# Sixteenth key tile of an attention head group: exponentials on VectorE instead of ScalarE, in a kernel of two attention layers and two token mixers

## The chip, the cores and the metric

The kernel runs on one core of a Trainium2 chip. The metric is the device time of one execution in microseconds. Six engines matter below. PE (TensorE) multiplies matrices and writes to PSUM, a memory of eight banks of 512 float32 columns on 128 partitions. ACT (ScalarE) and DVE (VectorE) work elementwise on PSUM and SBUF. POOL (GpSimd) works on SBUF and issues some DMAs, and SP (SyncE) issues the other DMAs. Each engine takes its instructions from a queue of its own, in order, and waits on semaphores that other engines set.

## The reference

```python
def _A_ref(x, wqkv, wo):              # B=1, S=2048, D=640, H=32, Dh=20
    qkv = ((x @ wqkv).reshape(B, S, 3, H, Dh)).transpose(2, 0, 3, 1, 4)
    q, k, v = qkv[0], qkv[1], qkv[2]
    scores = jnp.einsum("bhqd,bhkd->bhqk", q, k) * (Dh ** -0.5)
    p = _softmax(scores, axis=-1)
    o = jnp.einsum("bhqk,bhkd->bhqd", p, v)
    return o.transpose(0, 2, 1, 3).reshape(B, S, D) @ wo

def _B_ref(x, w1, b1, w2, b2):        # F=1536; mixes over the tokens
    h = _layernorm(x, axis=-1)
    u = _gelu(jnp.einsum("bsd,sf->bdf", h, w1) + b1)
    y = jnp.einsum("bdf,fs->bds", u, w2) + b2
    return y.transpose(0, 2, 1)

x = A_x
x = x + _A_ref(_layernorm(x), A_wqkv, A_wo)
x = x + _B_ref(_layernorm(x), B_w1, B_b1, B_w2, B_b2)
x = x + _A_ref(_layernorm(x), A_wqkv, A_wo)
x = x + _B_ref(_layernorm(x), B_w1, B_b1, B_w2, B_b2)
```

One attention layer needs 32 x 2048 x 2048 exponentials. The inputs are bfloat16.

## The kernel before

The program has four stages in a row: attention of layer 0, mixer 0, attention 1, mixer 1. The change touches the function `attention` and some constants at the top.

**Units and tiles.** The 32 heads are taken four at a time, in 8 head groups; the queries in 4 blocks of 512; the keys in 16 key tiles of 128. A unit is one (query block, head group, key tile), 512 units a layer. Each unit has four chunks, one for each head of the group: the scores of 128 keys by 512 queries, one PSUM bank. The chunks of all units, in order, are dealt out in threes to score tiles `S` of three banks; there are 683 of these a layer, and two buffers. The last tile of a layer has two chunks.

**What happens to a tile.** `emit_S` issues three matmuls, one a chunk. The head's 20 rows sit in one of four 32-row groups of PE (`tile_position`), and matmuls in different row groups run at the same time. `emit_exp` (line 322) takes the exponential of all three banks with one ACT instruction, [128, 1536], into a bfloat16 tile `P` (pool `ptp`, five buffers). No maximum is subtracted. `emit_PV` multiplies the four chunks of a unit with the values and adds them into the one `acc` bank over the 16 key tiles; the values carry a column of ones, which gives the softmax's denominators. After key tile 15, `normalize` (line 331) transposes `acc` on DVE in 32x32 blocks, takes reciprocals, multiplies and transposes back: four DVE instructions.

**The loop.** The loop at line 579 goes over the tiles. In iteration t it issues the scores of tile t+1, the exponential of tile t, the PV of every unit whose last chunk lies in tile t-1 or earlier, and then something to fill PE. `pe` (line 65) chains all PE instructions, so PE's order is the order of the program.

**What fills PE.** A queue of groups of matmuls holds the K and Q projections of the next head groups, the output projections and parts of the mixer's first matmul. `emit_fills` takes matmuls from it up to a budget: 3.0 of 512 columns in an iteration without PV, 1.5 in one with PV (the last may go over it, so two matmuls). A group writes the single `misc` bank; at its end DVE evacuates the bank, and for one iteration nothing is taken. For an output projection, the evacuation adds the residual, and after the second one of a row tile comes LN (`do_ln2`, line 357: two statistics, an aggregation, a small tensor-scalar, a power on POOL, an apply on DVE). In an iteration without fills, `keep_busy` (line 315) issues rounds of four matmuls with zero weights onto `acc`: SLOTS - 1 less the number of PVs.

**Order on the other engines.** The framework places the instructions of ACT, DVE, POOL and SP by data dependence and program order, and sets the semaphores. A tile's buffer is free for its next user when all its readers are done: a score tile when its exponential has read it.

Of the kernel before, what the change touches and what calls it, by code (L numbers as in the profile page):

```python
# [10 lines left out]

BF16 = mybir.dt.bfloat16
F32 = mybir.dt.float32
ACT = mybir.ActivationFunctionType
ALU = mybir.AluOpType
PSUM = bass.MemoryType.PSUM
# [5 lines left out]
NG = 8  # L22
# [6 lines left out]
    FILL_NOPV=3.0,  # L29
    FILL_PV=1.5,  # L30
    PV_LAGT=1,
    PT_BUFS=5,
    FILL_GAP=1,
    KQ_AHEAD=1,
    A0_LAG=2,
)


@with_exitstack
def kernel(  # L40
# [55 lines left out]
    nc.gpsimd.memset(zw[:], 0.0)  # L96
    zr = consts.tile([128, 512], BF16, name="zr")
    nc.gpsimd.memset(zr[:], 1.0)
    x1lp = ctx.enter_context(tc.tile_pool(name="x1lp", bufs=1))
    x1last = x1lp.tile([128, 4, D], F32, name="x1last")  # L100
    hhp = ctx.enter_context(tc.tile_pool(name="hhp", bufs=1))
# [141 lines left out]
    def attention(st, x_in_ap, x_mid, uacc_l):  # L243
        layer = st.layer
        KT, hT = st.KT, st.hT
        with ExitStack() as p1:
# [8 lines left out]
            h2_tiles = {}  # L255
            ptp = p1.enter_context(tc.tile_pool(name=f"ptp{layer}", bufs=CFG["PT_BUFS"]))
            atp = p1.enter_context(tc.tile_pool(name=f"atp{layer}", bufs=2))
            x1acc = {}
            LASTQB = NQB - 1
            PARTIAL_LAST = (NG % 2 == 0)  # L260
# [8 lines left out]
            tt_state = {}  # L269

            HORDER = (0, 1, 2, 3)
            chunks = [(n, j) for n in range(NU) for j in HORDER]
            NCH = len(chunks)
            NTILES = (NCH + 2) // 3

            def on_unit_start(n):
                qb_n, g_n, kt_n = units[n]
# [18 lines left out]
                if kt_n == 0:  # L296
                    ensure_ready(qb_n, g_n)

            def s_matmul(St, slot, n, j):
                qb, g, kt = units[n]  # L300
                pe(nc.tensor.matmul(St[:, slot, :], lhsT=KT[32 * j:32 * j + 32, g, kt * 128:(kt + 1) * 128],  # L301
                                    rhs=get_QT(st, qb)[32 * j:32 * j + 32, g, :], start=True, stop=True,
                                    tile_position=(32 * j, 0)))

            def emit_S(t):
                cs = chunks[3 * t:3 * t + 3]
                for (n, j) in cs:
# [4 lines left out]
                for i, (n, j) in enumerate(cs):  # L312
                    s_matmul(St, i, n, j)

            def keep_busy(count):
                for acc in acc_tiles.values():
# [4 lines left out]

            def emit_exp(t):
                St = S_tiles.pop(t)
                ncs = len(chunks[3 * t:3 * t + 3])
                P = ptp.tile([128, 3, 512], BF16, name="P")
                P_tiles[t] = P
                nc.scalar.activation(out=P[:, 0:ncs, :].rearrange("p a b -> p (a b)"),  # L327
                                     in_=St[:, 0:ncs, :].rearrange("p a b -> p (a b)"),
                                     func=ACT.Exp, scale=SCALE)
# [27 lines left out]
            def do_ln2(tt, x1s, engine):  # L357
                if tt >= 4 * MMO:
                    ln2_deferred.append((tt, x1s))
                    return  # L360
                mean, rstd = ln_stats(x1s[:], twice=True)
                h2t = h2sp.tile([128, D], BF16, name="h2st")
# [51 lines left out]
            def enqueue_outproj(qb):  # L414
                attnT = attnT_tiles[qb]
                for ttl in range(4):
                    tt = qb * 4 + ttl
                    for ci, (c0, c1) in enumerate(((0, 512), (512, D))):
                        w = c1 - c0
                        mms = []  # L420
                        for g in range(NG):
                            def mm(t, g=g, ttl=ttl, c0=c0, c1=c1, w=w, attnT=attnT, ci=ci, tt=tt):
                                if g == 0 and ci == 0:
                                    xin = xsp.tile([128, D], x_in_ap.dtype, name="xin")
                                    nc.sync.dma_start(out=xin[:], in_=x_in_ap[tt * 128:(tt + 1) * 128, :])
                                    tt_state[tt] = dict(xin=xin)
                                pe(nc.tensor.matmul(t[:, 0:w], lhsT=attnT[:, g, ttl * 128:(ttl + 1) * 128],  # L427
                                                    rhs=wo_pad[:, g, c0:c1], start=(g == 0), stop=(g == NG - 1)))
# [12 lines left out]
                        fill_queue.append(dict(mms=mms, evac=evac, cost=[1.0 if w > 256 else 0.35] * NG, key=("O", qb),  # L441
                                               not_before=fill_state["unit"] + 2))
# [73 lines left out]
            def emit_PV(n):  # L516
                qb, g, kt = units[n]
                if kt == 0:
                    acc_tiles[(qb, g)] = accp.tile([128, 512], F32, name="acc")
                acc = acc_tiles[(qb, g)]  # L520
                for j in range(4):
                    ci = 4 * n + HORDER.index(j)
                    P = P_tiles[ci // 3]
                    hh = 4 * g + j
                    pe(nc.tensor.matmul(acc[32 * j:32 * j + 32, :],  # L525
                                        lhsT=Vaug[:, (kt * H + hh) * VW:(kt * H + hh) * VW + 32],
                                        rhs=P[:, ci % 3, :], start=(kt == 0), stop=(kt == NKT - 1),
                                        tile_position=(0, 32 * j)))
                for t_ in list(P_tiles.keys()):
                    if (3 * t_ + 2) // 4 <= n:  # L530
                        del P_tiles[t_]
                if kt == NKT - 1:
                    normalize(qb, g, acc_tiles.pop((qb, g)))
                    if qb == LASTQB and PARTIAL_LAST:
                        if g % 2 == 1:
                            enqueue_outproj_partial(qb, g)
                    elif g == NG - 1:
                        enqueue_outproj(qb)

            def emit_fills(budget, pool_alloc):  # L540
# [5 lines left out]
                while spent < budget:  # L546
                    if fs["cur"] is None:
                        if not fill_queue:
                            break
                        if fill_queue[0].get("not_before", 0) > fs["unit"] and budget < 100:  # L550
                            break
                        fs["cur"] = fill_queue.popleft()
                        fs["idx"] = 0
                        fs["tile"] = pool_alloc()
                    grp = fs["cur"]
                    grp["mms"][fs["idx"]](fs["tile"])
                    spent += grp["cost"][fs["idx"]]
                    fs["idx"] += 1
                    if fs["idx"] == len(grp["mms"]):
                        grp["evac"](fs["tile"])  # L560
                        fs["cur"] = None
                        fs["cooldown"] = CFG["FILL_GAP"]
                        break
# [275 lines left out]
```

## Time and profile before

| | us |
|---|---|
| median of 3 runs | 2100.99 (2099.99 to 2101.32) |
| the profiled execution's own time | 2096.18 |
| its span, first to last instruction | 2094.4 |
| ACT busy | 1927.4 |
| of it line 327, the exponentials | 1835.9 |
| PE busy (its matmuls overlap; ends are modelled) | 1739.4 |
| DVE busy | 528.0 |
| POOL busy | 148.2 |

The profile gives busy time for each engine over one execution, groups of instructions by source line and shape, a chain of waits followed back from the last instruction, and the single instructions in order of time. The duration of an instruction in a group is from its own start to its own end; instructions that follow each other closely on one engine overlap, so that the busy time of a group is less than its count times its mean. The attention stages reach from about 49 to 963 us and from about 1090 to 2009 us; the mixers lie behind each. The granted PE clock was 0.985 on average.

### The profile page before, as it was taken

The numbers are of one execution on the slowest core, as the hardware profiler recorded it, in microseconds if no ns is written. First come the engines' busy times: TensorE is split into PE (matmuls) and PEld (weight loads), VectorE is DVE, ScalarE is ACT, GpSimd is POOL, SyncE is SP. The second block draws the span as 40 slices with busy tenths as digits, with TensorE's granted clock in tenths as the row PEclk, the third lists the DMA queues.
The fourth block names the chain that finished last, engine by engine and source line by source line (L and its number), as shares of the span: only waits on it lengthen the run. The fifth ranks groups of instructions, "written<-read, shape, count | busy, mean of one in ns | idle before, by whom it ended". The sixth has DMA issues, their size and how long they took to land.

```text
span 2094.4 us, 38271 instructions
## 1 busy us (share of the span) xinstructions
PE 1739.4 (83%) x16568; PEld 658.0 (31%) x16568; DVE 528.0 (25%) x1095; ACT 1927.4 (92%) x1504; POOL 148.2 (7%) x220
## 2 busy tenths in 40 slices
PE   7888888888888888887998888888888888878779
PEld 4222222232223322323542222222322223223235
DVE  6122222211321022213642122222112220322242
ACT  5999999999999999996449999999999999999962
POOL 2000000110012001110000000001100120011000
PEclk9999999999999999998999999999999999999999
DMA  5000000110034002223620000001101340132145
GB/s 130 1 1 1 1 20 20 61 54 11 29 59 71 2 29 43 41 30 106 221 85 1 1 1 1 26 27 66 48 14 39 65 65 1 52 53 38 20 140 182
DMA packets 90760, 97.27 MB, mean 46 GB/s; under 512 B 9696, under 2 KB 68192, under 8 KB 90592
## 3 DMA queue, kind: packets, MB, share of 16 engines
q1 hardware_dynamic: 70464, 71.22, 10.8%
q0 software_dynamic: 20128, 23.62, 7.5%
q8 instruction: 129, 2.11, 0.4%
q14 instruction: 39, 0.32, 0.0%
HBM read 55.48 MB, written 39.32 MB: 45 GB/s over the span
## 4 chain that ended last, share of the span: by engine, by line
ACT 68%; issue 17%; PE 12%; DVE 2%; DMA 1%; POOL 0%; SPq 0%; DVEq 0%; ACTq 0%; POOLq 0%
ACT P L327 67%; PE y L721 5%; PE S L301 1%; PE pp L217 1%; PE acc L525 1%; PE big L650 1%; PE misc L226 1%; DMA ua<-uacc 1%; PE misc L400 1%; PE acc L319 0%; PE pp L226 0%; PE S L460 0%; DMA x0in<-in_A_x_dram 0%; DVE bnst L157 0%; DVE x1last L473 0%
## 5 line engine op out<-in xcount | busy, mean ns | idle before, releaser
L327 ACT ACTIVATE P<-S 128x1536 bf16<-128x1536 f32 (+1 forms) x1366 | 1835.9, 1888 | 5.5 <-PE S L301 5.3
L301 PE MATMUL S<-QTq,KT 32*128 32x512 bf16 x4096 | 541.0, 383 | 314.0 <-ACT P L327 284.8
L301 PEld LDWEIGHTS <-KT 32*128 32x128 bf16 x4096 | 243.5, 91 | 796.5 <-issue 759.6
L525 PE MATMUL acc<-P,Vaug 128*32 128x512 bf16 x4096 | 414.1, 393 | 0.8 <-DVE T L336 0.5
L319 PE MATMUL acc<-zr,zw 128*32 128x512 bf16 x5208 | 390.5, 383 | 0.0
L525 PEld LDWEIGHTS <-Vaug 128*32 128x32 bf16 x4096 | 105.6, 93 | 235.9 <-issue 235.2
L319 PEld LDWEIGHTS <-zw 128*32 128x32 bf16 x5208 | 129.6, 96 | 90.9 <-issue 26.5
L406 DVE COPY ustg<-misc 128x512 f32<-128x512 f32 (+1 forms) x144 | 70.0, 486 | 335.6 <-PE misc L400 335.3
L336 DVE STREAM_TRANSPOSE T<-acc 128x512 f32<-128x512 f32 x64 | 45.8, 716 | 389.3 <-PE acc L525 389.1
L168 POOL TENSOR_TENSOR rstd<-veps,mhalf 128x1 f32<-128x1 f32 x64 | 35.4, 553 | 1180.0 <-DVE veps L163 1061.8
L400 PE MATMUL misc<-h2st,w1st 128*128 128x512 bf16 (+1 forms) x576 | 118.6, 308 | 0.0
L411 POOL DMA_DIRECT2D uacc<-ustg x96 | 82.6, 860 | 471.9 <-DVE ustg L406 443.0
L721 PE MATMUL y<-uT,w2s 128*128 128x512 bf16 (+1 forms) x768 | 107.7, 299 | 2.8 <-ACT uT L664 2.8
L487 DVE CAST QTq<-misc 128x512 bf16<-128x512 f32 x62 | 42.8, 691 | 243.3 <-PE misc L226 243.3
L226 PE MATMUL misc<-hh,wq_pad 128*128 128x512 bf16 x310 | 100.4, 391 | 0.0
L487 DVE CAST KT<-misc 128x512 bf16<-128x512 f32 x56 | 38.7, 690 | 217.9 <-PE misc L226 217.9
L226 PE MATMUL misc<-hh,wk_pad 128*128 128x512 bf16 x280 | 87.1, 385 | 0.0
L427 PE MATMUL misc<-wo_pad,attnT 128*128 128x512 bf16 (+1 forms) x384 | 77.3, 304 | 0.0
L721 PEld LDWEIGHTS <-w2s 128*128 128x128 bf16 x768 | 59.7, 98 | 49.1 <-issue 4.3
L76 ACT CAST Vaug<-pp 128x500 bf16<-128x500 f32 (+1 forms) x32 | 14.3, 452 | 51.3 <-PE pp L217 51.3
L436 DVE TENSOR_TENSOR x1s<-misc,xin 128x512 f32<-128x512 f32 (+1 forms) x48 | 23.5, 489 | 148.6 <-PE misc L427 148.5
L217 PE MATMUL pp<-wv,hh 128*128 128x500 bf16 (+1 forms) x320 | 50.4, 307 | 1.6 <-DVE hh L78 1.6
(76 smaller groups left out, 690.1 us busy)
## 6 DMA issues: line engine op xcount, KB each, us to landing
uacc<-ustg POOLq DMA_DIRECT2D x72, 256.0 KB, 4.0
w2s<-in_B_w_dram SPq DMA_DIRECT2D x16, 768.0 KB
w1st<-in_B_w_dram SPq DMA_DIRECT2D x36, 256.0 KB
xd<-x1s SPq DMA_DIRECT2D x24, 320.0 KB
x1in<-xd SPq DMA_DIRECT2D x24, 320.0 KB
ua<-uacc SPq DMA_DIRECT2D x24, 320.0 KB
xd<-x2s SPq DMA_DIRECT2D x16, 320.0 KB
xin<-xd SPq DMA_DIRECT2D x16, 320.0 KB
```

The lines of the kernel that those rows point to most:

```text
L217: pe(nc.tensor.matmul(pp[:, 0:c1 - c0], lhsT=st.hT[:, dt_, tt * 128:(tt + 1) * 128], rhs=wv[:, dt_, c0:c1], start=(dt_ == 0), stop=(dt_ == ...
L226: pe(nc.tensor.matmul(t[:, :], lhsT=wpad[:, dt_, g, :], rhs=st.hT[:, dt_, tb * 512:(tb + 1) * 512], start=(dt_ == 0), stop=(dt_ == NDT - 1)))
L301: pe(nc.tensor.matmul(St[:, slot, :], lhsT=KT[32 * j:32 * j + 32, g, kt * 128:(kt + 1) * 128], rhs=get_QT(st, qb)[32 * j:32 * j + 32, g, : ...
L319: pe(nc.tensor.matmul(acc[32 * j:32 * j + 32, :], lhsT=zw[:], rhs=zr[:], start=False, stop=False, skip_group_check=True, tile_position=(0, ...
L327: nc.scalar.activation(out=P[:, 0:ncs, :].rearrange("p a b -> p (a b)"), in_=St[:, 0:ncs, :].rearrange("p a b -> p (a b)"), func=ACT.Exp, ...
L400: pe(nc.tensor.matmul(t[:, 0:w], lhsT=states[fp]["w"][:, sti, ftl * 128:(ftl + 1) * 128], rhs=tiles4[sti][:, c0:c1], start=(sti == 0), sto ...
L406: nc.vector.tensor_copy(out=stg[:, 0:w], in_=t[:, 0:w])
L411: nc.gpsimd.dma_start(out=dst, in_=stg[:, 0:w], accum_op=ALU.add)
L427: pe(nc.tensor.matmul(t[:, 0:w], lhsT=attnT[:, g, ttl * 128:(ttl + 1) * 128], rhs=wo_pad[:, g, c0:c1], start=(g == 0), stop=(g == NG - 1)))
L487: nc.vector.tensor_copy(out=dst_ap, in_=t[:, :])
L525: pe(nc.tensor.matmul(acc[32 * j:32 * j + 32, :], lhsT=Vaug[:, (kt * H + hh) * VW:(kt * H + hh) * VW + 32], rhs=P[:, ci % 3, :], start=(kt ...
L721: pe(nc.tensor.matmul(y[:, 0:w], lhsT=w2s[:, ft, sl * 128:(sl + 1) * 128], rhs=uT[:, ft, c0:c1], start=(ft == 0), stop=(ft == NF - 1)))
```

## The change

In every head group and query block, key tile 15 (`VE_UNITS`) no longer goes to ACT. Its four chunks are put one by one into the third bank of score tiles early in the same group, three tiles apart (`VE_SPACING`); these mixed tiles have only two chunks for ACT, and `emit_exp` then covers two banks. In the mixed bank a matmul with constant weights `cw` first writes a bias, and the score matmul adds to it. DVE reads the bank once (`ve_first`): it multiplies by scale x log2(e) x 2^23, cuts at zero and writes int32. These bits, read as a float, hold the exponent. For each pair of such banks five more DVE instructions on 1024 columns follow (`ve_enqueue`): two bitwise ones separate mantissa and exponent, and three with two tensors evaluate a cubic polynomial of the mantissa, times the exponent, into a bfloat16 tile `Pd` that PV reads. They are held in a deque and issued by `ve_step` at an iteration's end, when an estimated clock of DVE says that it is free within 0.3 us; `ve_flush` issues what is left ahead of the unit's PV.

Besides, `P` has four buffers instead of five; next to mixed tiles one keep-busy round is left out, and the fill budget is 1.5; PV goes by the last tile of a unit (`last_tile`); and in layer 1 the sum `x1s` is written over the loaded residual `xin`.

```diff
-    PT_BUFS=5,
+    PT_BUFS=4,
+    VE_UNITS=((15,),),
+    VE_SPACING=3,
+    VE_SLACK=0.3,
...
+    ve_scale = SCALE * LOG2E
+    ve_bias = (127.0 + EXP_SHIFT) / ve_scale
+    cw = consts.tile([128, 128], BF16, name="cw")
+    nc.gpsimd.memset(cw[:], 0.0)
+    left = ve_bias
+    for row in (0, 32, 64):
...
+        nc.gpsimd.memset(cw[row:row + 1, :], part)
...
+            vew = p1.enter_context(tc.tile_pool(name=f"vew{layer}", bufs=2))
+            vet = p1.enter_context(tc.tile_pool(name=f"vet{layer}", bufs=1))
+            vep = p1.enter_context(tc.tile_pool(name=f"vep{layer}", bufs=2))
...
-            chunks = [(n, j) for n in range(NU) for j in HORDER]
...
+            act_chunks = deque((n, j) for n in range(NU) for j in HORDER if not is_ve[n])
...
+            while act_chunks or ve_queue:
+                if act_chunks:
+                    qb_, g_, _ = units[act_chunks[0][0]]
+                    if seen_group != (qb_, g_):
+                        seen_group = (qb_, g_)
+                        n0 = (qb_ * NG + g_) * NKT
+                        ve_queue += [(n0 + kt, j) for kt in ve_kts(qb_, g_) for j in HORDER]
+                t = len(tiles)
+                ve = None
+                na = 3
+                if ve_queue and t - last_mixed >= CFG["VE_SPACING"]:
+                    js = {c[1] for c in list(act_chunks)[:2]}
+                    ve = next((c for c in ve_queue if c[1] not in js), ve_queue[0])
+                    ve_queue.remove(ve)
+                    last_mixed = t
+                    na = 2
+                acts = [act_chunks.popleft() for _ in range(min(na, len(act_chunks)))]
...
+            def ve_first(p, slot, St):
+                if slot == 0:
+                    ve_w[p] = vew.tile([128, 2, 512], I32, name="ew")
+                nc.vector.tensor_scalar(out=ve_w[p][:, slot, :], in0=St[:, 2, :], scalar1=ve_scale * 2.0 ** 23,
+                                        scalar2=0.0, op0=ALU.mult, op1=ALU.max)
+                dve_cost(0.69)
+                if slot + 1 == len(ve_pairs[p]):
+                    ve_enqueue(p)
+
+            def ve_enqueue(p):
...
+                def mant():
+                    box["m"] = vet.tile([128, 1024], I32, name="em")
+                    nc.vector.tensor_scalar(out=box["m"][:, 0:512 * k], in0=wi, scalar1=0x007FFFFF, scalar2=0x3F800000,
+                                            op0=ALU.bitwise_and, op1=ALU.bitwise_or)
...
+                def expo():
+                    nc.vector.tensor_scalar(out=wi, in0=wi, scalar1=0x7F800000, scalar2=None, op0=ALU.bitwise_and)
+
+                def p1_():
+                    box["t"] = vet.tile([128, 1024], F32, name="et")
+                    nc.vector.scalar_tensor_tensor(out=box["t"][:, 0:512 * k], in0=box["mf"], scalar=EXP_A, in1=box["mf"],
+                                                   op0=ALU.add, op1=ALU.mult)
...
+                    nc.vector.scalar_tensor_tensor(out=t, in0=t, scalar=EXP_B, in1=box["mf"], op0=ALU.add, op1=ALU.mult)
...
+                    Pd = vep.tile([128, 2, 512], BF16, name="Pd")
+                    ve_P[p] = Pd
+                    nc.vector.scalar_tensor_tensor(out=Pd[:, 0:k, :].rearrange("p a b -> p (a b)"),
+                                                   in0=box["t"][:, 0:512 * k], scalar=EXP_C, in1=wf,
+                                                   op0=ALU.add, op1=ALU.mult)
+                for cost, fn in ((0.69, mant), (0.69, expo), (1.22, p1_), (1.22, p2_), (1.22, p3_)):
+                    ve_chain.append((p, cost, fn))
+
+            def ve_step(us):
+                ve_clock["now"] += us
+                while ve_chain and ve_clock["free"] <= ve_clock["now"] + CFG["VE_SLACK"]:
+                    p, cost, fn = ve_chain.popleft()
+                    fn()
+                    dve_cost(cost)
...
             def emit_S(t):
...
                 St = sps.tile([128, 3, 512], F32, name="S")
                 S_tiles[t] = St
+                if ve is not None:
+                    pe(nc.tensor.matmul(St[:, 2, :], lhsT=cw[:], rhs=zr[:], start=True, stop=False,
+                                        skip_group_check=True))
+                for i, (n, j) in enumerate(acts):
                     s_matmul(St, i, n, j)
+                if ve is not None:
+                    s_matmul(St, 2, ve[0], ve[1], start=False)
+                    ve_first(*loc[ve], St)
...
-                                ts_["x1s"] = xsp.tile([128, D], F32, name="x1s")
+                                ts_["x1s"] = (ts_["xin"] if x_in_ap.dtype == F32 else
+                                              xsp.tile([128, D], F32, name="x1s"))
...
+                if is_ve[n]:
+                    ve_flush(n)
                 for j in range(4):
-                    ci = 4 * n + HORDER.index(j)
-                    P = P_tiles[ci // 3]
+                    ti, slot = loc[(n, j)]
+                    P = ve_P[ti] if is_ve[n] else P_tiles[ti]
...
-                while pv_done < NU and (4 * pv_done + 3) // 3 <= t - LAGT:
+                while pv_done < NU and last_tile[pv_done] <= t - LAGT:
...
+                short = len(tiles[t][0]) < 3
+                extra = 1 if t + 1 < NTILES and tiles[t + 1][1] is not None else 0
                 if not has_fill:
-                    keep_busy(CFG["SLOTS"] - 1 - n_pv)
-                emit_fills(CFG["FILL_PV"] if n_pv else CFG["FILL_NOPV"], misc_alloc)
+                    keep_busy(CFG["SLOTS"] - 1 - n_pv - extra - short)
+                emit_fills(CFG["FILL_PV"] if n_pv or extra or short else CFG["FILL_NOPV"], misc_alloc)
+                ve_step(0.92 if short else 1.344)
```

More of the change, by code (lines that the diff above doesn't have):

```diff
@@ L13 @@
 F32 = mybir.dt.float32
+I32 = mybir.dt.int32
 ACT = mybir.ActivationFunctionType
@@ L35 @@
     A0_LAG=2,
-)
+    VE_UNITS=((15,),),
+    VE_SPACING=3,
+    VE_SLACK=0.3,
+)
+LOG2E = 1.4426950408889634
+EXP_C3 = 0.07802455
+EXP_A = -0.00800647 / EXP_C3
+EXP_B = 0.47777278 / EXP_C3
+EXP_C = 0.45213437 / EXP_C3
+EXP_SHIFT = float(np.log2(EXP_C3))
 @with_exitstack
@@ L98 @@
     nc.gpsimd.memset(zr[:], 1.0)
+    ve_scale = SCALE * LOG2E
[4 more added lines that the diff above has]
+    for row in (0, 32, 64):
+        part = float((np.asarray(left, np.float32).view(np.uint32) & np.uint32(0xFFFF0000)).view(np.float32))
+        nc.gpsimd.memset(cw[row:row + 1, :], part)
+        left -= part
     x1lp = ctx.enter_context(tc.tile_pool(name="x1lp", bufs=1))
@@ L271, in attention, with ve_kts @@
             HORDER = (0, 1, 2, 3)
-            chunks = [(n, j) for n in range(NU) for j in HORDER]
-            NCH = len(chunks)
-            NTILES = (NCH + 2) // 3
+            def ve_kts(qb, g):
+                pat = CFG["VE_UNITS"]
+                return pat[(qb * NG + g) % len(pat)]
+            is_ve = [kt in ve_kts(qb, g) for (qb, g, kt) in units]
+            tiles, loc, last_tile = [], {}, {}
+            ve_queue, ve_pairs = [], []
+            act_chunks = deque((n, j) for n in range(NU) for j in HORDER if not is_ve[n])
@@ new lines, in attention @@
+            last_mixed = -CFG["VE_SPACING"]
+            seen_group = None
+            while act_chunks or ve_queue:
[15 more added lines that the diff above has]
+                acts = [act_chunks.popleft() for _ in range(min(na, len(act_chunks)))]
+                for i, c in enumerate(acts):
+                    loc[c] = (t, i)
+                    last_tile[c[0]] = t
+                if ve is not None:
+                    if not ve_pairs or len(ve_pairs[-1]) == 2:
+                        ve_pairs.append([])
+                    loc[ve] = (len(ve_pairs) - 1, len(ve_pairs[-1]))
+                    ve_pairs[-1].append(ve)
+                    last_tile[ve[0]] = t
+                tiles.append((acts, ve))
@@ new lines, in attention, with dve_cost @@
+            NTILES = len(tiles)
+            ve_w, ve_P = {}, {}
+            ve_chain = deque()
+            ve_clock = dict(now=0.0, free=0.0)
+            def dve_cost(us):
+                ve_clock["free"] = max(ve_clock["free"], ve_clock["now"]) + us
+            def ve_first(p, slot, St):
[6 more added lines that the diff above has]
+                    ve_enqueue(p)
@@ new lines, in ve_enqueue, with p2_, p3_ @@
+            def ve_enqueue(p):
+                k = len(ve_pairs[p])
+                w = ve_w.pop(p)
+                wi = w[:, 0:k, :].rearrange("p a b -> p (a b)")
+                wf = wi.bitcast(F32)
+                box = {}
+                def mant():
+                    box["m"] = vet.tile([128, 1024], I32, name="em")
+                    nc.vector.tensor_scalar(out=box["m"][:, 0:512 * k], in0=wi, scalar1=0x007FFFFF, scalar2=0x3F800000,
+                                            op0=ALU.bitwise_and, op1=ALU.bitwise_or)
+                    box["mf"] = box["m"][:, 0:512 * k].bitcast(F32)
+                def expo():
[4 more added lines that the diff above has]
+                                                   op0=ALU.add, op1=ALU.mult)
+                def p2_():
+                    t = box["t"][:, 0:512 * k]
+                    nc.vector.scalar_tensor_tensor(out=t, in0=t, scalar=EXP_B, in1=box["mf"], op0=ALU.add, op1=ALU.mult)
+                def p3_():
+                    Pd = vep.tile([128, 2, 512], BF16, name="Pd")
[5 more added lines that the diff above has]
+                    ve_chain.append((p, cost, fn))
@@ new lines, in ve_step, with ve_flush @@
+            def ve_step(us):
[4 more added lines that the diff above has]
+                    dve_cost(cost)
+            def ve_flush(n):
+                need = {loc[(n, j)][0] for j in HORDER}
+                while any(c[0] in need for c in ve_chain):
+                    p, cost, fn = ve_chain.popleft()
+                    fn()
+                    dve_cost(cost)
@@ L297, in on_unit_start, with s_matmul @@
                     ensure_ready(qb_n, g_n)
-            def s_matmul(St, slot, n, j):
+            def s_matmul(St, slot, n, j, start=True):
                 qb, g, kt = units[n]
                 pe(nc.tensor.matmul(St[:, slot, :], lhsT=KT[32 * j:32 * j + 32, g, kt * 128:(kt + 1) * 128],
-                                    rhs=get_QT(st, qb)[32 * j:32 * j + 32, g, :], start=True, stop=True,
-                                    tile_position=(32 * j, 0)))
+                                    rhs=get_QT(st, qb)[32 * j:32 * j + 32, g, :], start=start, stop=True,
+                                    skip_group_check=not start, tile_position=(32 * j, 0)))
             def emit_S(t):
-                cs = chunks[3 * t:3 * t + 3]
-                for (n, j) in cs:
+                acts, ve = tiles[t]
+                for (n, j) in acts:
                     if j == HORDER[0]:
@@ L311, in emit_S @@
                 S_tiles[t] = St
-                for i, (n, j) in enumerate(cs):
+                if ve is not None:
+                    pe(nc.tensor.matmul(St[:, 2, :], lhsT=cw[:], rhs=zr[:], start=True, stop=False,
+                                        skip_group_check=True))
+                for i, (n, j) in enumerate(acts):
                     s_matmul(St, i, n, j)
+                if ve is not None:
+                    s_matmul(St, 2, ve[0], ve[1], start=False)
+                    ve_first(*loc[ve], St)
             def keep_busy(count):
@@ L323, in emit_exp @@
                 St = S_tiles.pop(t)
-                ncs = len(chunks[3 * t:3 * t + 3])
+                ncs = len(tiles[t][0])
+                if ncs == 0:
+                    return
                 P = ptp.tile([128, 3, 512], BF16, name="P")
@@ L361, in do_ln2 @@
                 mean, rstd = ln_stats(x1s[:], twice=True)
+                dve_cost(2.0)
                 h2t = h2sp.tile([128, D], BF16, name="h2st")
@@ L526, in emit_PV @@
                                         lhsT=Vaug[:, (kt * H + hh) * VW:(kt * H + hh) * VW + 32],
-                                        rhs=P[:, ci % 3, :], start=(kt == 0), stop=(kt == NKT - 1),
+                                        rhs=P[:, slot, :], start=(kt == 0), stop=(kt == NKT - 1),
                                         tile_position=(0, 32 * j)))
-                for t_ in list(P_tiles.keys()):
-                    if (3 * t_ + 2) // 4 <= n:
-                        del P_tiles[t_]
+                if not is_ve[n]:
+                    for t_ in list(P_tiles.keys()):
+                        if tiles[t_][0][-1][0] <= n:
+                            del P_tiles[t_]
                 if kt == NKT - 1:
                     normalize(qb, g, acc_tiles.pop((qb, g)))
+                    dve_cost(2.4)
                     if qb == LASTQB and PARTIAL_LAST:
@@ L560, in emit_fills @@
                         grp["evac"](fs["tile"])
+                        dve_cost(grp.get("dve", 0.69))
                         fs["cur"] = None
```

## The prediction

> **What bounds the kernel now.** I read the page's busy shares first, then its groups by shape, the chain, the waits, the busy time by stretch, and last two stretches of the timeline.
>
> ```profile
> PE 1739.4 (83%) x16568; PEld 658.0 (31%) x16568; DVE 528.0 (25%) x1095; ACT 1927.4 (92%) x1504; POOL 148.2 (7%) x220
> ...
> ACT 68%; issue 17%; PE 12%; DVE 2%; DMA 1%; POOL 0%; SPq 0%; DVEq 0%; ACTq 0%; POOLq 0%
> ```
> ```profile
> L327 ACT ACTIVATE P<-S 128x1536 bf16<-128x1536 f32 x1364 | 1834.1, 1888 | 5.5 <-PE S L301 5.3
> ...
> L341 DVE TENSOR_TENSOR T<-T,rden 128x512 bf16<-128x512 f32 x64 | 44.2, 691 | 2.1
> ...
> L487 DVE CAST KT<-misc 128x512 bf16<-128x512 f32 x56 | 38.7, 690 | 217.9 <-PE misc L226 217.9
> ...
> L173 DVE TENSOR_SCALAR h2st<-x1s,mv,rstd 128x640 bf16<-128x640 f32 x24 | 14.7, 613 | 17.5 <-POOL rstd L168 17.5
> ...
> L76 ACT CAST Vaug<-pp 128x500 bf16<-128x500 f32 x19 | 10.7, 574 | 25.8 <-PE pp L217 25.8
> ...
> L76 ACT CAST Vaug<-pp 128x140 bf16<-128x140 f32 x13 | 3.6, 275 | 25.4 <-PE pp L217 25.4
> ...
> L327 ACT ACTIVATE P<-S 128x1024 bf16<-128x1024 f32 x2 | 3.2, 1597 | 0.0
> ```
> ```profile
> PE S L301 <- ACT P L327: 284.8, 937, 0.9
> ```
> ```profile
> 280.00:510.00 230.00, 191.26 (x1903) 67.74 (x1901) 48.43 (x94) 229.40 (x172) 15.20 (x28) 0.99 0.11 35
> ```
> The exponentials own the two attention stages: 1366 of them keep ACT busy 1835.9 us, 1.344 us a tile (their 1888 ns overlap), and they wait 5.5 us in all. PE waits for them 937 times. The last row holds a stretch's length and then PE, weight loads, DVE, ACT and POOL: ACT has 229.4 of 230 us, DVE 48.4. Over the eight attention stretches read so, DVE has 387.6 of 1828 us, 21%. What ACT loses in work here comes off the end, as long as PE and DVE keep up.
>
> PE's room shows in this stretch (start, length):
> ```profile
> 515.23 0.39 PE L301 MATMUL S<-QTq,KT 32*128 32x512 bf16 x3
> 515.55 0.10 PEld L525 LDWEIGHTS <-Vaug 128*32 128x32 bf16 x4 [0.23 <-issue]
> 515.55 0.40 PE L525 MATMUL acc<-P,Vaug 128*32 128x512 bf16 x4
> 515.88 0.11 PEld L427 LDWEIGHTS <-attnT 128*128 128x128 bf16 x2 [0.23 <-issue]
> 515.88 0.60 PE L427 MATMUL misc<-wo_pad,attnT 128*128 128x512 bf16 x2
> 516.42 0.23 PEld L301 LDWEIGHTS <-KT 32*128 32x128 bf16 x3 [0.42 <-issue]
> ```
> From start to start: scores 0.32, PV 0.33, two fill matmuls 0.54, together 1.19 of 1.344 us. Elsewhere in that stretch three fills take 0.76 and two keep-busy rounds with their PV 0.76.
>
> **Removed: ACT work.** Counting through the new tile loop: still 683 tiles a layer, but 128 are mixed, with two banks for ACT and one for DVE. Both layers lose 512 columns from 256 exponentials. What is 512 columns worth? The two casts give (574-275)/360 = 0.83 ns a column, 0.425 us; a third of the period would be 0.448; the 1024-wide exponentials are 0.291 shorter by the means, and 0.467 by their minimum (1445 ns) against the median (1912 ns). The casts' slope is the only one free of queueing, so 0.425: 256 x 0.425 = 108.8 us (ends 74.5 and 119.6). A short exponential then takes 0.92 us.
>
> **Added: DVE work.** For each mixed tile one read of a score bank, 0.69 by the KT cast, same shape and source. For each pair of such tiles five operations on 1024 columns. The three with two tensors: the 512-column tensor-tensor row is 0.691; between the 512 and 128-column copies out of PSUM (0.685, 0.288) lies 1.03 ns a column, so 0.691 + 0.53 = 1.22. The two bitwise ones have no row. The nearest is the f32 tensor-scalar, 0.613 for 640: unchanged it bounds them below, the two-tensor 1.22 above; scaled by columns it gives 0.98, and I take 0.80. A pair: 2 x 0.69 + 2 x 0.80 + 3 x 1.22 = 6.64 us (6.27 to 7.48); 128 pairs: 850 us. With the 387.6 that is 1238 us in some 1730 us of attention: 72% (69 to 78). It fits, beside ACT.
>
> The Trainium skill, "ScalarE: Activation LUTs", Rules for kernel authors, speaks against the change: for exp, ScalarE is the only option. The rows bear out that DVE is the dear place, 3.3 us a bank against 0.43 on ACT; by the rule the sum would be 256 x (3.3 - 0.43), 735 us worse, were both on one path. They aren't: ACT is full and DVE 79% idle.
>
> **Added: waits on DVE's queue.** The bank read waits for its score matmul, and evacuations, normalize and LN stand behind it. S two tiles later waits for it. Scores of mixed tile m start when exponential m-2 ends and the banks are needed again 1.344 + 0.92 = 2.26 us later. Bias and scores take 0.71, the read 0.69: 0.86 us spare before PE is held, and about 0.85 more (1.344 less S's 0.39 and a handover) before ACT runs dry. A chain operation in front (1.22) fits into 1.71. What does not: LN of a row tile (two statistics 0.98, aggregation 0.20, veps 0.15, POOL 0.55, apply 0.61, handovers: some 3 us behind its 0.69 evacuation). Of the 12 a layer, two stand one tile ahead of a mixed one: 4 x 1.5 = 6 us at most. Normalize always stands two tiles ahead; its transpose frees the only acc buffer, and a chain operation in front makes the next PV late by up to 1.22, mostly within S's spare. A late misc evacuation holds the next fill: at 1135.05 it starts 2.59 us ahead of that fill, so 1.9 spare, 1.5 with a short tile between. For all of this 5 us (0 to 30).
>
> The skill's "SBUF — State Buffer", on the shared port of DVE and GpSimd, says that a two-port DVE operation shuts POOL out of writing DMA descriptors for its whole length; no run here shows it. Counted as 0.8 us for each of the 144 uacc issues that is 115 us on POOL, which is 7% busy, and nothing at the end.
>
> **Added: PE work.** A bias matmul in front of the scores (0.22 after a fill, 0.32 after keep-busy, by the steps above), and in 64 of the 128 tiles the DVE bank shares its row group with one of the other two, so the three no longer run at once: 0.22. Taken off: keep-busy rounds next to mixed tiles. Counting iterations through the loop, a layer: ahead of a mixed tile 25 with fills alone (1.08), 33 with fills and PV (1.41), 69 without fills (1.17 to 1.19), and 0.11 for the shared row groups: 1.33 on average; at the mixed one 58 at 1.19, 18 with two PVs at 1.42, 52 with one keep-busy round or none at 0.86: 1.09; all others 1.08 to 1.19: 1.11. Three in a row: 3.53 us against ACT's 2 x 1.344 + 0.92 = 3.61. With fills in two of the three (79 of 127 cycles) PE needs 1.52 + 1.19 + 1.08 = 3.79, 0.18 too much; four such cycles make 0.7 a head group, about what S's spare holds, and nine unmixed tiles follow that give back 0.2 each. With fills in all three (10 cycles) it is 0.3 too much. If nothing came back: 2 x (79 x 0.18 + 10 x 0.3) = 34 us; if all did, 0. I take 8.
>
> **PT_BUFS 5 to 4.** Exponential t+4 waits for the PV of the last unit in P tile t. Normally that is two tiles earlier. Only where a unit spans a mixed tile and both its neighbours (40 a layer) does PV end some 1.0 us into a period of 1.344; with PE 0.3 late it ties. 80 x 0 to 0.3: take 3 (0 to 24).
>
> **Edits at nothing.** Three pools are SBUF only. The cw fills are four POOL memsets (0.2 for the ident-sized one, 0.12 each at most for one row); POOL waits 5.02 us before its first rstd, which hides them; bare they cost 0.6. x1s on top of xin in layer 1 keeps a buffer until LN is done; loads alternate over two, a row tile is many periods long, so 0 (at most 2). No DMA is added or moved on SP's or POOL's queue, and the clock variables only set where the chain is issued. A second PV at the end: 0.3 a layer.
>
> **Sum.** -108.8 + 5 + 8 + 3 + 0.6 = -92 us. The profiled execution took 2096.18 us, 1.8 over its 2094.4 span: 2094.4 - 92 = 2002, 2004 with what lies around it. The median shown, 2100.99, is 4.8 higher: 2009 us.
>
> **Rivals.**
> - PE becomes the bound in the fill stretches and the short exponential saves only 0.291: 74.5 - 34 - 10 = about 30 us left, 2070. For it: the 3.79 against 3.61. Against it: PE's counted total of 783 us a layer against ACT's 863.
> - DVE's queue holds the scores (slower). Place: the bank read behind two or more chain operations, since the chain is issued by an estimated clock that knows none of DVE's waits. It eats the whole gain from a mean lateness of 1.71 + 0.43 = 2.1 us at each mixed tile. At 2.5 (two operations of 1.22) ACT stalls 0.8 x 256 = 205 us: 2101 + 96 = about 2197. Against it: 72% load, and one operation in front is harmless.
> - Nothing changes, 2101: the losses equal the gain, or shorter exponentials don't shorten ACT's period. Against it: ACT's wait of 5.5 us.
>
> **How the numbers follow.** My forecast (1984 to 2040): 0.71. The first rival, between 2040 and 2096: 0.15. Within 0.2%, about what this kernel's measurement can tell from no change: 0.02. DVE's queue: 0.12. Faster is 0.86. The low end is 2101 - 119.6 with 2.6 lost. The high end, 2055, takes seven tenths of the losses' upper bounds together (0.7 x (30 + 34 + 24) = 62, off 108.8), and reaches so far into the first rival that a third of it (0.05), DVE's queue and no change (0.14) stay outside.
>
> **What would show it.** Right: 256 1024-wide exponentials, ACT busy in line 327's successor at about 1727 us with idle before them under 20 us, DVE near 65%, score matmuls that still wait for ACT and hardly for DVE. Wrong: exponentials that wait for scores by tens of us, scores that wait for the new DVE read, or bitwise operations above 1.22 us.

## The result, and the profile after

The changed kernel takes 2190.46 us in the median (2188.24 to 2191.22), against 2100.53 for the one before: a ratio of 1.0426, 95% interval 1.0408 to 1.0444. It was forecast at 2009 and is 90 us slower than the kernel before. The profiled execution took 2189.74 us, its span is 2187.7.

Busy time and the chain's shares by engine, from the page of the changed kernel:

```profile
PE 1843.8 (84%) x16632; PEld 634.1 (29%) x16632; DVE 1292.6 (59%) x1991; ACT 1845.7 (84%) x1504; POOL 153.2 (7%) x224
...
ACT 30%; DVE 24%; PE 23%; issue 21%; DMA 1%; POOL 0%; ACTq 0%; SPq 0%; DVEq 0%; POOLq 0%
```

The exponentials as a whole, in the kernel before and in the changed one (count | busy us, mean ns | idle us before and what ended it):

```profile
L327 ACT ACTIVATE P<-S 128x1536 bf16<-128x1536 f32 (+1 forms) x1366 | 1835.9, 1888 | 5.5 <-PE S L301 5.3
```
```profile
L457 ACT ACTIVATE P<-S 128x1536 bf16<-128x1536 f32 (+1 forms) x1366 | 1753.9, 1398 | 176.7 <-DVE ew L344 160.5
```

Groups by shape of the changed kernel (lines of `ve_first` are L344, of the chain's five operations L359 to L378):

```profile
L457 ACT ACTIVATE P<-S 128x1536 bf16<-128x1536 f32 x1108 | 1516.4, 1485 | 5.6 <-PE S L423 4.4 <-PE acc L659 0.9
...
L457 ACT ACTIVATE P<-S 128x1024 bf16<-128x1024 f32 x258 | 264.5, 1025 | 171.2 <-DVE ew L344 160.5 <-DVE mv L180 2.9 <-PE misc L531 2.4
L344 DVE TENSOR_SCALAR ew<-S 128x512 int32<-128x512 f32 x256 | 174.3, 681 | 395.1 <-PE S L423 394.8
L373 DVE SCALAR_TENSOR_TENSOR et<-et,em 128x1024 f32<-128x1024 f32 x128 | 156.3, 1221 | 2.8
...
L364 DVE TENSOR_SCALAR ew<-ew 128x1024 int32<-128x1024 int32 x128 | 89.2, 697 | 4.0
L359 DVE TENSOR_SCALAR em<-ew 128x1024 int32<-128x1024 int32 x128 | 88.3, 690 | 3.2
```

ACT does have less to do. But DVE has come into the chain, 24% against 2%, and the short exponentials stand idle for 171.2 us before they start, nearly always for `ew`, DVE's read of the third bank of their own tile. The waits say it in one line, 248 of the 256:

```profile
ACT P L457 <- DVE ew L344: 160.5, 248, 2.0
```

The account closes on the rows of the exponentials as a whole. Their busy and idle time was 1835.9 + 5.5 = 1841.4 us; now it is 1753.9 + 176.7 = 1930.6, 89.2 more, and the span has grown by 93.3. Had they kept ACT full, 108.8 fewer than before would be about 1727 busy. So 171 us of the missing time is new idle time, and 27 is overlap lost: an exponential after a wait doesn't overlap the one before (the short ones' busy time, 264.5 us, is their count times their mean).

One mixed tile in the timeline (start, length; the idle time before and what ended it in brackets):

```profile
504.82 0.38 PE L435 MATMUL S<-zr,cw 128*128 128x512 bf16 x1 [0.19 <-ACT P L457]
...
505.12 0.39 PE L423 MATMUL S<-QTq,KT 32*128 32x512 bf16 x3
...
505.56 0.69 DVE L344 TENSOR_SCALAR ew<-S 128x512 int32<-128x512 f32 x1 [10.26 <-PE S L423]
...
506.35 3.71 ACT L457 ACTIVATE P<-S 128x1024 bf16<-128x1024 f32 x3 [0.24 <-DVE ew L344]
```

DVE had been free for 10.26 us and read at once. Still ACT waited: from the bias matmul to the exponential, bias, scores and read take 506.35 - 504.82 = 1.53 us. With 0.05 us between the end of the exponential two tiles earlier and the bias matmul that is 1.58, and the exponential that runs meanwhile covers 1.344 of it. A wait of 0.24 us is left where nothing is late; not all are so short (median 0.46 us, 66 of 256 over 1 us).

Why does the exponential wait for a read of another bank? The trace's semaphores say it: all 256 exponentials of mixed tiles wait for a semaphore of DVE, while those of three banks wait for PE's.

Here the framework puts the two readers of one PSUM tile, which are on different engines, one after the other in program order, though they read different banks; and the read stands in `emit_S`, ahead of the exponential. The first two experiments below test this.

### The profile page after: what moved, and what is told of

Same layout as the page of the kernel before. It is cut to its first block, busy times and chain, and to the rows that moved or that the text cites. A ratio compares the mean times of both kernels' runs of the same rounds, so it can differ in the third digit from the quotient of the medians.

```text
span 2187.7 us, 39310 instructions
## 1 busy us (share of the span) xinstructions
PE 1843.8 (84%) x16632; PEld 634.1 (29%) x16632; DVE 1292.6 (59%) x1991; ACT 1845.7 (84%) x1504; POOL 153.2 (7%) x224
## 4 chain that ended last, share of the span: by engine, by line
ACT 30%; DVE 24%; PE 23%; issue 21%; DMA 1%; POOL 0%; ACTq 0%; SPq 0%; DVEq 0%; POOLq 0%
ACT P L457 29%; PE S L423 6%; DVE ew L344 5%; PE y L861 4%; PE acc L659 3%; DVE et L368 3%; DVE et L373 3%; PE S L435 2%; DVE attnT L473 2%; DVE em L359 2%; DVE T L466 2%; PE misc L246 2%; DVE T L471 2%; DVE ew L364 1%; PE pp L237 1%
## 5 line engine op out<-in xcount | busy, mean ns | idle before, releaser
L457 ACT ACTIVATE P<-S 128x1536 bf16<-128x1536 f32 (+1 forms) x1366 | 1753.9, 1398 | 176.7 <-DVE ew L344 160.5
L423 PE MATMUL S<-QTq,KT 32*128 32x512 bf16 x4096 | 577.1, 390 | 239.8 <-ACT P L457 220.6
L423 PEld LDWEIGHTS <-KT 32*128 32x128 bf16 x4096 | 210.0, 91 | 831.1 <-issue 802.4
L344 DVE TENSOR_SCALAR ew<-S 128x512 int32<-128x512 f32 x256 | 174.3, 681 | 395.1 <-PE S L423 394.8
L373 DVE SCALAR_TENSOR_TENSOR et<-et,em 128x1024 f32<-128x1024 f32 x128 | 156.3, 1221 | 2.8
L378 DVE SCALAR_TENSOR_TENSOR Pd<-et,ew 128x1024 bf16<-128x1024 f32 x128 | 155.7, 1216 | 1.0
L368 DVE SCALAR_TENSOR_TENSOR et<-em 128x1024 f32<-128x1024 f32 x128 | 155.7, 1216 | 0.0
L435 PE MATMUL S<-zr,cw 128*128 128x512 bf16 x256 | 98.4, 384 | 58.6 <-ACT P L457 54.5
L542 POOL DMA_DIRECT2D uacc<-ustg x96 | 86.2, 898 | 470.9 <-DVE ustg L537 454.3
L246 PE MATMUL misc<-hh,wq_pad 128*128 128x512 bf16 x310 | 93.3, 384 | 0.0
L364 DVE TENSOR_SCALAR ew<-ew 128x1024 int32<-128x1024 int32 x128 | 89.2, 697 | 4.0
L359 DVE TENSOR_SCALAR em<-ew 128x1024 int32<-128x1024 int32 x128 | 88.3, 690 | 3.2
```

The lines of the kernel that those rows point to most:

```text
L246: pe(nc.tensor.matmul(t[:, :], lhsT=wpad[:, dt_, g, :], rhs=st.hT[:, dt_, tb * 512:(tb + 1) * 512], start=(dt_ == 0), stop=(dt_ == NDT - 1)))
L344: nc.vector.tensor_scalar(out=ve_w[p][:, slot, :], in0=St[:, 2, :], scalar1=ve_scale * 2.0 ** 23, scalar2=0.0, op0=ALU.mult, op1=ALU.max)
L359: nc.vector.tensor_scalar(out=box["m"][:, 0:512 * k], in0=wi, scalar1=0x007FFFFF, scalar2=0x3F800000, op0=ALU.bitwise_and, op1=ALU.bitwise_or)
L368: nc.vector.scalar_tensor_tensor(out=box["t"][:, 0:512 * k], in0=box["mf"], scalar=EXP_A, in1=box["mf"], op0=ALU.add, op1=ALU.mult)
L373: nc.vector.scalar_tensor_tensor(out=t, in0=t, scalar=EXP_B, in1=box["mf"], op0=ALU.add, op1=ALU.mult)
L378: nc.vector.scalar_tensor_tensor(out=Pd[:, 0:k, :].rearrange("p a b -> p (a b)"), in0=box["t"][:, 0:512 * k], scalar=EXP_C, in1=wf, op0=AL ...
```

## The experiments

Theory A: this wait is the loss. Rival B: DVE comes late to the read, because of what its queue holds, and the wait only shows it.

**The wait taken away.** The edge between the two readers is left out; the exponential waits for its own scores instead, and the next scores in the buffer for both readers. The two touch different banks, so nothing is shared.

```diff
+                if t in ve_rd:
+                    tc.declare_no_dep(ex.ins, ve_rd[t].ins, reason="other banks of the tile")
+                    for m_ in ve_mm[t]:
+                        tc.add_manual_dep(ex.ins, m_.ins.name, sync_dep, reason="scores")
...
+                if t - 2 in ve_rd:
+                    for m_ in first:
+                        tc.add_manual_dep(m_.ins, ve_rd[t - 2].ins.name, sync_dep, reason="bank read by DVE")
```

> The changed kernel, but the two-bank exponential no longer waits for DVE's read of the third bank of its score tile; it waits for its own scores, and the next scores in that buffer wait for both readers. Theory A (the exponential's wait for the read is the loss: it puts bias, scores and read in a row between two exponentials): the 160.5 us that exponentials wait for the read go to 0, their idle time falls from 177 us to under 30, no new wait of that size comes up, and the time is 2000 to 2030 us. Rival B (DVE is late because of what its queue holds ahead of the read; the wait only shows it): the wait moves on to the scores two tiles later, some 100 us or more of scores waiting for the read or of exponentials waiting for scores, and the time stays above 2100 us.

Measured: 2026.51 us, ratio to before 0.9644 (0.9621 to 0.9667). The exponentials, and the waits that are left:

```profile
L465 ACT ACTIVATE P<-S 128x1536 bf16<-128x1536 f32 (+1 forms) x1366 | 1739.7, 1448 | 29.9 <-PE S L426 22.0
```
```profile
PEld L426 <- DVE ew L346: 77.7, 119, 1.5
...
PE S L426 <- DVE ew L346: 24.1, 52, 1.1
```

A holds. Without the one wait the same instructions are 164 us faster and beat the kernel before. Of B a part is left: weights and scores of the tile two further on do wait for the read, 102 us in all, but the exponentials wait for scores for 22 us only, and the time is far from B's.

**The read issued after the exponential.** The edge turns round.

```diff
-                    ve_first(*loc[ve], St)      # at the end of emit_S
...
+                if tiles[t][1] is not None:      # at the end of emit_exp
+                    ve_first(*loc[tiles[t][1]], St)
```

> The changed kernel with the DVE read issued after the tile's exponential instead of before it, so that DVE waits for ACT instead of ACT for DVE. Theory A: the exponentials' wait for the read is gone, but the bank is held until the exponential's end, then 0.1 + 0.69 + 0.1 for the read and 0.39 + 0.1 for the next scores, 1.4 us against the 1.344 us exponential that runs meanwhile; a prompt read costs about nothing and DVE's lateness (0.38 us in the mean over the 0.27 us floor of the waits now) goes straight to ACT: 2101 - 109 + 15 + 95 = about 2100 us, 2060 to 2130. Rival B: no better than now, 2170 us or more.

Measured: 2111.32 us, ratio 1.0049 (1.0033 to 1.0065), within A's range and far from B's. By the trace's semaphores all 256 reads now wait for ACT, so the order did follow the program; the scores two tiles later wait for `ew`:

```profile
PE S L423 <- DVE ew L344: 123.5, 206, 1.9
...
ACT P L456 <- PE S L423: 68.1, 168, 1.4
```

**The chain left out, twice.** To split a prompt read from a late one, the read writes straight into PV's tile and the five chain operations go. These exponentials of key tile 15 are left out, then. This run and the other three without the chain, and the later one without the bias matmul, were measured once each; the kernel before, run beside them, lay between 2097 and 2107 us.

```diff
-                    ve_w[p] = vew.tile([128, 2, 512], I32, name="ew")
-                nc.vector.tensor_scalar(out=ve_w[p][:, slot, :], in0=St[:, 2, :], scalar1=ve_scale * 2.0 ** 23,
+                    ve_P[p] = vep.tile([128, 2, 512], BF16, name="Pd")
+                nc.vector.tensor_scalar(out=ve_P[p][:, slot, :], in0=St[:, 2, :], scalar1=0.001,
...
-                if slot + 1 == len(ve_pairs[p]):
-                    ve_enqueue(p)
```

> The changed kernel without the five chain operations for each pair of banks: the read scales the scores straight into the bfloat16 tile that PV uses, so these exponentials are left out. The exponential still waits for the read. Theory A: the read is prompt now, but 0.24 to 0.28 us of wait for each of 256 tiles stays, because bias, scores and read follow each other: 60 to 70 us of ACT waiting for the read, and 2080 to 2105 us. Rival B: with nothing of the chain ahead of the read the whole gain comes back, 2000 to 2030 us.

> Both of the above: no chain (the exponentials of key tile 15 are left out, the read goes straight to PV's tile) and no wait of the exponential for the read. This measures what the shorter exponentials are worth with PE's added work alone. Both theories: exponentials idle under 15 us, time 1990 to 2010 us. If it stays above 2030, PE's added matmuls are a bound that neither theory has.

Measured: 2268.45 us with the wait and 2020.74 without it. Both lie above every range given, and the edit is why: the read now needs a buffer of `Pd`, of which there are two, and waited for the last head group's PV, 375 us in the first (below) and 371 us in the second.

```profile
DVE Pd L344 <- PE acc L657: 374.7, 60, 18.3
...
ACT P L455 <- DVE Pd L344: 239.1, 253, 2.4
```

It splits nothing, but shows the mechanism once more: whatever holds the read holds ACT. Both were repeated with four buffers of `Pd`.

> The run without the chain again, with four buffers of Pd instead of two. In the first such run the read wrote straight into Pd and had to wait for the PV of the group before (375 us of DVE waiting for PV), which the exponential then waited for as well. With four buffers that is gone. The exponentials of key tile 15 are left out; the exponential still waits for the read. Theory A (the wait itself, with bias, scores and read in a row): about 0.27 us for each of 256 tiles, 60 to 80 us, remain, and with them 2070 to 2105 us. Rival B (only what the queue holds ahead of the read): 2000 to 2030 us.

> No chain, no wait of the exponential for the read, four buffers of Pd: the shorter exponentials with PE's added work and the bare read alone (the exponentials of key tile 15 are left out). The earlier run had 2021 us, with 371 us of DVE waiting for PV and 86 us of score weights waiting for the read. Both theories: those waits gone, 2000 to 2015 us. What the kernel with the chain but without the wait (2026.5) lies above it is the price of the chain on DVE's queue, expected 10 to 25 us.

Measured: 2136.52 us with the wait, 1995.63 without. The exponentials in the first and in the second, and the wait in the first:

```profile
L455 ACT ACTIVATE P<-S 128x1536 bf16<-128x1536 f32 (+1 forms) x1366 | 1752.2, 1401 | 123.9 <-DVE Pd L344 121.0
```
```profile
L463 ACT ACTIVATE P<-S 128x1536 bf16<-128x1536 f32 (+1 forms) x1366 | 1732.3, 1495 | 5.5 <-PE S L424 2.4
```
```profile
ACT P L455 <- DVE Pd L344: 121.0, 254, 2.2
```

So the wait costs 141 us even where nothing of the chain is ahead of the read: 118 in idle time (123.9 against 5.5) and 20 in overlap lost (the exponentials' busy time 1752.2 against 1732.3). That is more than A said, and the second run is a little faster than its range. The waits fall into two heaps in the timeline, 77 at 0.2 to 0.3 us and 120 at 0.3 to 0.5, median 0.44: where the DVE bank shares its row group with one of the other two (half of the tiles), its score matmul runs after it, some 0.22 us later, and the read with it. The expectation had 0.27 for all. Another 57 are longer than 0.5 us, 36 of them because the read starts late after all, over 0.15 us behind its scores; DVE still has its evacuations and normalize.

In steps, each a difference of two runs: 2100.5 less 104.9 (shorter exponentials, with PE's work: 1995.6) plus 141 (the wait) plus 54 (the chain, while the wait is there: 2190.5 against 2136.5). Of the 54, about 41 is lateness: reads start 0.30 us after their scores in the mean in the changed kernel, and 0.14 here. The mean clock also differs (0.970 against 0.987); what that is worth was not measured. Without the wait the chain costs 31 (2026.5 against 1995.6).

**PE's bias matmul left out**, on the kernel without the wait.

```diff
-                    first.append(pe(nc.tensor.matmul(St[:, 2, :], lhsT=cw[:], rhs=zr[:], start=True, stop=False,
-                                                     skip_group_check=True)))
...
-                    s_matmul(St, 2, ve[0], ve[1], start=False)
+                    s_matmul(St, 2, ve[0], ve[1])
```

> The kernel without the wait, and without the bias matmul in front of the scores of mixed tiles (the exponents of key tile 15 lack their bias, so these probabilities come out as about zero). It prices PE's added matmul. By the prediction's sum all of PE's added work cost 8 us: 2016 to 2024 us. If the rest of the lost gain (2026.5 against 2101 - 109 = 1992) is PE's, 2010 or less.

Measured: 2011.91 us, 14.6 less: between the two guesses. The matmul makes the read ready 0.3 us later (505.12 - 504.82 above), and DVE's lateness would count from there; that this is the way it costs is argued, not shown.

**Mixed tiles four and five apart**, without the wait, and with only the matmul into the third bank ordered behind the read.

```diff
-    VE_SPACING=3,
+    VE_SPACING=4,          # the next run: 5
...
-                    for m_ in first:
+                    for m_ in first[2:3]:
```

> The kernel without the wait, with mixed tiles four apart instead of three, and with only the score matmul that writes the third bank ordered behind the read. DVE's work for a group spreads over 16 tiles instead of 12. If what is left (78 us of score weights and 24 us of scores waiting for the read, 30 us of exponentials idle) comes from chain operations ahead of the read, these waits halve and the time is 2010 to 2022 us; if it comes from PE's added work, 2023 to 2030.

> Without the wait, mixed tiles five apart: DVE's work for a group spreads over some 16 to 20 of 21 tiles, and none of the 128 DVE banks of a layer shares its row group with a neighbour (64 with three apart, 10 with four). If spreading the chain goes on helping, 1996 to 2003 us; but the last chain of a group then ends only about when its PV is due, and if PV waits for it, 2005 to 2020.

Measured: 2004.86 us (ratio 0.9543, 0.9527 to 0.9559) and 1989.37 us (0.9468, 0.9454 to 0.9482), both faster than expected. With five apart almost nothing is left of any wait:

```profile
L465 ACT ACTIVATE P<-S 128x1536 bf16<-128x1536 f32 (+1 forms) x1366 | 1727.3, 1570 | 4.2 <-PE S L426 4.2
```
```profile
PEld L426 <- DVE ew L346: 6.0, 13, 0.6
```

PV did not wait for the last chain, as had been feared. Several things go together here: the chain spread over more tiles, fewer shared row groups (64, 10 and 0 of 128 a layer), and from three to four apart also the looser order behind the read. One more run takes them apart a little: four apart, but only at tiles where a row group is free.

```diff
-                    ve = next((c for c in ve_queue if c[1] not in js), ve_queue[0])
+                    ve = next((c for c in ve_queue if c[1] not in js), None)
+                    if ve is None and t - last_mixed >= CFG["VE_SPACING"] + 2:
+                        ve = ve_queue[0]
```

> Without the wait, mixed tiles at least four apart and only where one of the DVE banks left has a free row group (none shares now; the kernel with four apart has 10 of 128 that do). Ten fewer score matmuls of 0.22 us in a row, twice: at most 4 us. 2000 to 2005 us, not to be told from the kernel with four apart (2004.9).

Measured: 2002.47 us (0.9528, 0.9511 to 0.9545), no difference from 2004.86 that could be told. From four to five apart it isn't the shared row groups, then, and the spreading is what is left. From three to four apart these causes weren't separated.

**Five apart with the wait left in**: the changed kernel with that one number changed.

> The changed kernel with mixed tiles five apart and nothing else: the exponential still waits for the read. It tells whether the wait or the spacing made the loss. Theory A (the wait): no row group is shared, so every prompt wait is the 0.24 to 0.27 us floor, 65 us, plus 20 us of overlap between exponentials lost, on top of 1989: 2075 to 2100 us. If spacing was the cause and the wait only its sign, 1990 to 2020 us.

Measured: 2097.16 us, ratio 0.9984 (0.9975 to 0.9994), within the range that A gave.

```profile
L457 ACT ACTIVATE P<-S 128x1536 bf16<-128x1536 f32 (+1 forms) x1366 | 1752.4, 1382 | 87.7 <-DVE ew L344 86.1
```
```profile
ACT P L457 <- DVE ew L344: 86.1, 256, 1.9
```

All 256 exponentials of mixed tiles wait, 202 of them 0.24 us, though DVE reads promptly (233 reads within 0.15 us of their scores' end) and no row group is shared. Against 1989.37 the wait costs 108 us here, by itself just about the whole gain: 83.5 us more idle time and 25 us of overlap lost. Against the changed kernel, the wider spacing alone is worth 93 us. This is the version that settles it: spacing mends the lateness, and only taking the wait away gives the gain. The best kernel is the one without the wait and with mixed tiles five apart, 1989.37 us, 5.3% under the kernel before.

## Why the prediction was wrong

**The step that failed** is "Added: waits on DVE's queue". It said of the read that "S two tiles later waits for it", worked out 1.71 us to spare from that, and took 5 us (0 to 30). The exponential of the same tile waits for it too. There is then no spare at all: bias, scores and read have to fit under one exponential, and they miss it by 0.24 us where nothing is late (0.44 with a shared row group). Measured: 141 us with nothing of the chain ahead of the read and 54 more with it, 195 in place of 5. I took the two readers for independent because their banks are; whether the program orders them was never asked, and the trace of before doesn't show it: its score tiles have one reader, the exponential.

**The rival that came closest** in time, "DVE's queue holds the scores", about 2197 us, has the engine right and the place wrong. The chain ahead of the read, its cause, is worth 54 us of the 195. It was to decide from a mean lateness of 2.1 us; in fact the read may be on time and the gain is gone (2097.16 with five apart). The chance of 0.12 was for another mechanism, and that its 2197 lies near the 2190 measured is luck.

**ACT's saving**, 108.8 us by the casts' slope: right. With next to no waits (five apart) the exponentials' busy time is 1727.3 us against 1835.9, 108.6.

**DVE's operations.** Read 0.681 us (0.69 forecast), three-operand ones 1.22 (1.22), both right. The bitwise ones 0.690 and 0.697, where I took 0.80 between 0.613 and 1.22. The Trainium skill, "VectorE: DVE Perf Modes", The perf-mode tier table, gives an fp32 tensor_scalar in SBUF two columns a cycle, and these int32 rows agree (0.69 against 1.22 for two tensors). DVE's busy time grew by 765 us, where the sum had 850: the bitwise operations were taken 0.1 us too long each, and operations that follow each other overlap. It did fit beside ACT.

**PE's added work**, 8 us (0 to 34): all of PE's work and the bare reads cost 108.8 - 104.9 = 4 us (the run without chain and wait, measured once). The bias matmul is worth 14.6 us with the chain on, more than was put down for all of PE's work.

**Chain without the wait**: 31 us at three apart, just over my 0 to 30. At five apart the kernel with the chain is 6 us faster than the one without it at three. So the forecast of 2009 was 17 us short of the same kernel without the wait (2026.5), mainly for this reason, and the larger error is the wait.

**PT_BUFS**, 3 us (0 to 24): 5.1 us of exponentials waiting for PV in the kernel without the wait. Right.

**The shared port of DVE and GpSimd** (the skill's "SBUF — State Buffer"): the 96 longer uacc issues took 898 ns each against 860 before, 86.2 against 82.6 us together, where the page's rule for all 144 was counted as 115. Few of them meet a bitwise operation: 16 of the 96 ran at the same time as one and lasted 1.05 us in the mean (up to 1.17), the other 80 lasted 0.87. So what meets does get longer, as the page has it, and it comes to little because it seldom meets. That the port is the reason isn't shown.

**What would show it**: "exponentials that wait for scores by tens of us, scores that wait for the new DVE read" was the list of wrong signs. The sign that came, exponentials that wait for the read itself, isn't on it.

## What to carry to other kernels

Before moving part of a buffer's work to a second engine, look up in the program's waits how the framework orders the two readers: an order between reads of different banks can cost as much as the move brings. Price a new wait at every reader and writer of the tile, the tile's own next step first, and only then at the buffer's next user. When a helper engine has long operations, spread its work evenly: here, without the wait, five tiles apart in place of three took 37 us off (2026.5 to 1989.4), together with fewer shared row groups and the looser order.

## What the runs showed of the hardware

- An exponential that starts after a wait costs more than its wait. A [128, 1024] one lasts 1025 ns by itself, and back to back about 0.92 from end to end (five apart, without the wait); over some 255 breaks the busy time was 20 us longer (1752.2 against 1732.3).
- PE's granted clock can halve without a long pause. In the changed kernel, the stretches 508 to 510, 510 to 512 and 512 to 514 us (length, PE, weight loads, DVE, ACT, POOL, then the clock):

```profile
508.00:510.00 2.00, 1.24 (x12) 0.28 (x12) 1.93 (x4) 2.00 (x2) 0.00 (x0) 1.00 0.00 0
510.00:512.00 2.00, 1.90 (x17) 0.37 (x14) 1.93 (x4) 1.76 (x3) 0.00 (x0) 0.54 0.00 0
512.00:514.00 2.00, 2.00 (x18) 0.50 (x16) 1.97 (x2) 2.00 (x2) 0.00 (x0) 0.60 0.00 0
```

  PE was 62% busy in the first, with one wait of 0.95 us, and had 0.54 and 0.60 of the clock in the next two; scores took 0.61 us in place of 0.39. The Trainium skill, "TensorE: Matmul & The Clock Gate", Part 1, has the clock drop after an idle window of about 3.4 us; no such pause is in this stretch. The same Part also tells of a kernel in which PE idles briefly between groups of matmuls so often that the clock goes up and down; this stretch is nearer to that. The lower clock may add to the loss here, but doesn't make it: without the chain the wait cost 141 us at a mean clock of 0.987, against 0.985 before.
